# Multi-head attention and an expert layer on one core: all attention first, and seven products instead of eight in the first expert matmul of four batches

## The chip, the core and the metric

The kernel runs on one core of a Trainium2 chip. The core has a matrix engine (TensorE, PE below), a vector engine (VectorE, DVE), a scalar engine that evaluates functions (ScalarE, ACT), a general engine (GpSimd, POOL) that here issues the input transfers, and a queue engine (SyncE, SP) that issues output transfers. They run side by side and wait for each other through semaphores. Matmuls write to PSUM banks; DVE and ACT read them. The metric is the device time of one execution in microseconds (us).

## What is computed

The inputs are q, k, v of 8 batches, 12 heads, 448 tokens and 64 numbers per head, in float32, and two weight matrices, 768 x 2048 and 2048 x 768. Cut to what matters:

```python
scores = q @ k.T / sqrt(64)                 # per batch and head, 448 x 448
attn = exp(scores - max); attn /= sum(attn) # softmax over keys
x = (attn @ v), heads side by side          # 3584 x 768
h = x @ w_in                                # 3584 x 2048, "first expert matmul"
out = (h * sigmoid(h)) @ w_out              # 3584 x 768,  "second expert matmul"
```

h * sigmoid(h) is the function Silu. The matmuls run in float16 with float32 accumulation.

## The kernel before

**Attention.** The 12 heads of a batch are three head groups of four. A *unit* is a batch and a head group (batch 0 is cut into two pieces of tokens as well), 27 units in all. K and Q are loaded per unit, turned by DVE (`turn_k`, `turn_q`), and `scores` multiplies 128 keys at a time with 448 queries on 32-row tiles of PE into a pair of PSUM banks of the ring "s" (two pairs). `expo` (L386) lets ACT write the exponentials to a tile E (nine buffers). `attend` (L412) multiplies them with V, and `attend_sums` (L428) with ones for the softmax's denominators, on 32-column tiles. DVE turns and inverts the sums (`inverse`: sT, inv, rdn) and `norm` (L486) writes xT, half the normalised result, in transposed form.

**First expert matmul.** For batches 0 to 5, `ffn1` multiplies one block of 128 columns of w_in with xT: six products over the 768 rows, 448 tokens wide. ACT takes tanh of it (`tanh`, L511; buffers "th", three) and DVE makes (tanh + 1) * h/2 (`gate`, L546), which is Silu. For batches 6 and 7 together (`PB = B - 2`) it is done as a 2 x 2 block product with seven block products instead of eight (`queue_pair`, `pair_product`): the two batches are the rows, the two halves of the columns the columns, the two halves of the 768 the inner index. For each pair of column blocks f and f + 8 there are seven block products of three matmuls each. Sums of blocks of xT (sx, `combine_x`, L592) and of w_in (tw, `combine_w_in`, L610) are made by DVE before, copies of two intermediate results by ACT (`pair_copy`, L647), three additions by DVE (`pair_add`, L650), and ACT's Silu (`silu`, L659) reads the four results. Tanh and exponential share one function table of ACT, Silu needs another; `first_silu` (L656) brings the load forward.

**Second expert matmul.** For every two tiles of 128 tokens (a *quad*, `queue_quad`) it is also a 2 x 2 block product in seven parts (`product`): DVE makes the sums S and in-place differences in G (`combine_g`, L683), ACT copies (L751), DVE adds (L758, L763), ACT or DVE write the result to ost, and SP stores it (in the last quads ACT's queue too). The first quad is done in four plain products (`plain`).

**Column strips.** While attention runs, `wide` (L337) cuts each 128-column product of the expert layer into four strips of 32 columns, which saves a change of tiling between it and the attention products.

**Order.** Nothing is left to an automatic scheduler. A planner in the kernel (`Order`, `Op`, `Ring`) goes through a clock of estimated durations. DVE and ACT take the operation that has been ready longest, corrected by a `bias`; PE takes a score when its operands and buffers are free and `PACE` us have passed since the last (L1475), else expert work from a list `moe`, of which the first 24 entries are looked through (`moe_ready`), or attention products (`av_at`, `run_av`). Buffers are rings in the planner ("m": four single PSUM banks; "s"; E; V; raw K and Q; turned K; T; S; tmp; ost). The buffers "th" have no ring in it. All loads go through POOL's one queue in a fixed order, and one that waits for its buffer holds back those behind it. V lies in two buffers of a whole batch each.

Of the kernel before, what the change touches and what calls it, by code (L numbers as in the profile page):

```python
# [174 lines left out]
def kernel(  # L175
# [28 lines left out]
    NRK, NRQ = 3, 4  # L204
    PACE = 2.6
# [6 lines left out]
    SHY = 0.5  # L212
    TWB, SXB = 4, 4
    PIECES = ((0, 7), (7, TPP))
    NE, NX3, NT_ = 9, 6, 2
# [32 lines left out]
    VT = [const.tile([128, NH, NCH, D], FP16, name=f"V{i}") for i in range(2)]  # L248

    def clear_v(i, hg, low):  # L250
        rows = slice(64, 128) if low else slice(0, 64)
        nc.vector.memset(VT[i][rows, HG * hg : HG * (hg + 1), NCH - 1], 0.0)

    for hg in (1, 2):
        clear_v(1, hg, hg == 1)
# [26 lines left out]
    def load_v(b, hg0, hg1, x):  # L282
        hs = slice(HG * hg0, HG * hg1)
        first, count = X_TOK[form(b, hg0)][x]
        nc.gpsimd.dma_start(  # L285
            out=VT[b % 2][32 * x : 32 * (x + 1), hs, 0:count, :],
            in_=v[b, hs].rearrange("h (i g) d -> i h g d", g=TPP)[
                :, :, first : first + count, :
            ],
        )  # L290
# [16 lines left out]
    def turn_k(b, hg):  # L307
        t = rawk[(b, hg)][:].bitcast(FP32).rearrange("p (g i) -> p g i", i=32)
        kt = sb.tile([128, NCH, 4, 32, 2], FP16, name=f"KT_{b}_{hg}", tag="KT", bufs=3)
# [94 lines left out]
    def attend_mm(a, n, part, c, h, k0, k1, e, start, stop):  # L404
# [3 lines left out]
        if part == 0:  # L408
            w = ones[k0:k1, :]
        else:  # L410
            w = VT[b % 2][k0:k1, HG * hg + h, c, part - 1 :: 2]
# [24 lines left out]
    def attend(ns, part):  # L436
        lone = len(ns) == 1
        if part == 0 and not lone:
            attend_sums(ns)
            return  # L440
        for n in ns:
            a = ps.tile([128, 512], FP32, name=f"a_{n}_{part}", tag="m", bufs=4)
            acc[(n, part)] = a
            for c in range(NCH):
                e = E[(ns[0] if c == NCH - 1 else n, c // per_burst(n))]
                for h in range(HG):
                    attend_mm(
                        a, n, part, c, h, 0, rows_of(n, c), e, c == 0, c == NCH - 1
                    )

    def inverse(ns, step, i=0):
        g0, g1 = units[ns[0]][2:]
        shape = [128, g1 - g0, 32]
        if step == 0:
            sT_t[ns[0]] = sb.tile(shape, FP32, name=f"sT_{ns[0]}", tag="sT", bufs=1)
# [41 lines left out]
    def ffn1(b, f, t0, t1):  # L497
        h = ps.tile([128, 512], FP32, name=f"h_{b}_{f}_{t0}", tag="m", bufs=4)
        for cc in range(NDC):
# [7 lines left out]
        h_t[(b, f, t0)] = h  # L507

    def tanh(b, f, t0, t1):
        th = sb.tile([128, t1 - t0], FP16, name=f"th_{b}_{f}_{t0}", tag="th", bufs=3)  # L510
# [29 lines left out]
    def gate(b, f, t0, t1):  # L540
        r = b % 2
        cut = 6 * 128 - S if b % 4 == 1 else S
        for lo, hi, dst, at in ((0, cut, G, S * r), (cut, S, X, -cut)):
# [21 lines left out]
    PB = B - 2  # L565
    c_t, sx_t, tw_t, pp_t, pf_t = {}, {}, {}, {}, {}

    def old_buffer(name, home, cols):

        if home == "V":  # L570
            t = VT[name[:2] == "sx"].rearrange("p h c d -> p (h c d)")
        else:
            t = sb.tile([128, HG, S], FP16, name=name, tag="E", bufs=NE)
            t = t.rearrange("p h s -> p (h s)")
        return [
            t[:, 3 * cols * i : 3 * cols * (i + 1)].rearrange("p (c t) -> p c t", c=3)
            for i in range(2 if home == "V" else 1)
        ]

    def combine_x(m):  # L580
        if m < 4:
            made = old_buffer(f"sx_{m}", "V" if m == 3 else "E", S)
            for i, t in enumerate(made):
                sx_t[m + i] = t
        x = {(r, i): x3(PB + r, 3 * i) for r in range(2) for i in range(2)}
        a, b, op = {
            1: (x[1, 0], x[1, 1], ALU.add),
            2: (sx_t.get(1), x[0, 0], ALU.subtract),
            3: (x[0, 0], x[1, 0], ALU.subtract),
            4: (x[0, 1], sx_t.get(2), ALU.subtract),  # L590
        }[m]
        nc.vector.tensor_tensor(out=sx_t[m], in0=a, in1=b, op=op)  # L592
# [5 lines left out]
    def combine_w_in(m, f0):  # L598
        if (m, f0) not in tw_t:
            made = old_buffer(f"tw_{m}_{f0}", W_HOME.get((m, f0), "E"), 512)  # L600
            for i, t in enumerate(made):
                tw_t[(m + i, f0)] = t
        x = {(i, j): w_in_part(i, j, f0, f0 + 4) for i in range(2) for j in range(2)}
        a, b, op = {
            1: (x[0, 1], x[0, 0], ALU.subtract),
            2: (x[1, 1], tw_t.get((1, f0)), ALU.subtract),
            3: (x[1, 1], x[0, 1], ALU.subtract),
            4: (x[1, 0], tw_t.get((2, f0)), ALU.subtract),
        }[m]
        nc.vector.tensor_tensor(out=tw_t[(m, f0)], in0=a, in1=b, op=op)  # L610

    W_HOME = {(1, 0): "V"}
    PBANK = {1: "A", 2: "A", 6: "B", 7: "B", 4: "B", 5: "C", 3: "C"}

    def pair_product(f, m):
        if m in (1, 5):
            pp_t[(f, PBANK[m])] = ps.tile(
                [128, 512], FP32, name=f"f_{f}_{m}", tag="m", bufs=4
            )[:, 0:S]
        elif m == 6:  # L620
            two = ps.tile([128, 2, 512], FP32, name=f"f_{f}_{m}", tag="s", bufs=2)
            pp_t[(f, "B")], pp_t[(f, "D")] = two[:, 0, 0:S], two[:, 1, 0:S]
        x = {(r, i): x3(PB + r, 3 * i) for r in range(2) for i in range(2)}
        lo, at = f // 4 * 4, slice(128 * (f % 4), 128 * (f % 4 + 1))
# [3 lines left out]
            3: (sx_t.get(4), w_in_part(1, 1, f, f + 1)),  # L628
        }.get(m, (None, None))
        if a is None:  # L630
            i = {4: 4, 5: 1, 6: 2, 7: 3}[m]
            a, w = x[1, 1] if m == 4 else sx_t[i], tw_t[(i, lo)][:, :, at]
        for c in range(3):
            wide(
# [8 lines left out]
    def pair_copy(f, name, at):  # L643
        tag, n = {"p": ("rq", NRQ), "q": ("rk", NRK)}[name]
        t = sb.tile([128, TPP * D], FP16, name=f"{name}_{f}", tag=tag, bufs=n)
# [12 lines left out]
    def silu(f, r, x):  # L658
        nc.scalar.activation(  # L659
            out=G[:, f, S * r : S * (r + 1)],  # L660
            in_=pp_t[(f % HF, x)],
            func=AF.Silu,
            scale=2.0,
        )
# [22 lines left out]
    def product(qd, m):  # L687
# [6 lines left out]
        if BANK[m] == m:  # L694
            pr_t[(qd, m)] = ps.tile([128, 512], FP32, name=f"p_{qd}_{m}", tag="m", bufs=4)
        for f in range(HF):
# [80 lines left out]
    rk_ring, rq_ring, v_ring = Ring(NRK), Ring(NRQ), Ring(2)  # L777
    kt_ring, t_ring = Ring(3), Ring(NT_)
# [11 lines left out]
    def plan_v(b, hg0, hg1):  # L790
        made = []
        for x in range(4):
            ring = v_ring if (x == 0 and hg0 == 0) else None
# [79 lines left out]
    quads, fourth = [], []  # L873

    def queue_ffn1(b, g0, g1):
        t0, t1 = 32 * g0, 32 * g1
        for f in range(NFF) if b == 0 else [x for f in range(HF) for x in (f, f + HF)]:

            def run(f=f):
                op = Op("PE", NDC * mm(t1 - t0), lambda: ffn1(b, f, t0, t1), tail=PE_OUT)  # L880
# [4 lines left out]
                od.on_pe(op, "full")  # L885
# [31 lines left out]
    pair_todo = [(m, f0) for f0 in (0, 4) for m in (1, 2, 3, 4)]  # L917

    def plan_pair():
        while pair_todo and not od.pool:  # L920
            m, f0 = pair_todo[0]
            if (m, f0) in W_HOME:
                if not v_ring.can(1, od.now):
                    return
                v_ring.take()
            elif (m - 1, f0) not in W_HOME:
                if qk_seq or not e_ring.can(1, od.now):
                    return
                e_ring.take()
            pair_todo.pop(0)  # L930
            pair_w[(m, f0)] = od.add(
                Op(
                    "DVE",
                    0.98,
                    lambda m=m, f0=f0: combine_w_in(m, f0),
                    [pair_w[(k, f0)] for k in {2: (1,), 4: (2,)}.get(m, ())],
                    TWB + f0,
# [3 lines left out]
    def queue_pair():  # L941
        xs = {(r, c): x_op[(PB + r, c, 0)] for r in range(2) for c in range(NDC)}
        v_ring.take()
        e_ring.take(2)
        od.add(
            Op(
                "ACT",
                2.7,
# [597 lines left out]
```

## Time and profile before

| | |
|---|---|
| time, median of 3 runs | 394.65 us (394.5 to 394.73) |
| the profiled execution: time / span | 394.84 / 392.9 us |
| mean granted clock of PE | 0.999 |
| busy: PE, DVE, ACT, POOL | 386.2, 274.1, 253.1, 83.6 us |
| idle of ACT before E, most of it for scores | 22.5 us |
| ACT's second table load | 1.28 us, at 300 us |
| last attention product / first seven-product work | about 303.7 / 316.0 us |

The span runs from the first to the last instruction. A line of a group gives the line in the kernel, engine, operation, what it writes and reads, shape, count, then busy time and mean length of one in ns, and the engine's idle time before them with what ended it. The chain is the work that ended last, followed back. PE's ends are modelled, and instructions of an engine that follow each other closely overlap, so that mean lengths add up to more than the busy time.

### The profile page before, as it was taken

The page shows a single profiled execution, that of the slowest core. Times are in us where ns is not written, and L with a number is a line of the kernel's source. Part 1 is how long each engine was busy: PE and PEld are TensorE (multiplying, and loading weights), DVE is VectorE, ACT ScalarE, POOL GpSimd, SP SyncE. Part 2 cuts the span into 40 slices and gives each one's busy share as a digit, 9 for nine tenths or more (in the row PEclk, how much of TensorE's full clock was granted, in tenths as well). Part 3 has the DMA queues.
Part 4 walks back from the last instruction along what each step waited for, and adds up shares of the span by engine and source line. Part 5 has one row for each costly group of instructions (what it writes and reads, how often), then busy time and mean ns, then how long its engine had stood idle before and what let it go on. Part 6 is the DMA issues. An engine that isn't in the chain of part 4 may idle for free.

```text
span 392.9 us, 14583 instructions
## 1 busy us (share of the span) xinstructions
PE 386.2 (98%) x6343; PEld 213.1 (54%) x6343; DVE 274.1 (70%) x576; ACT 253.1 (64%) x404; POOL 83.6 (21%) x153
## 2 busy tenths in 40 slices
PE   8999999999999999999999999999999999999995
PEld 7667774444556444555455544445445555555663
DVE  3477676999967488964699576996879945457332
ACT  4988885596872886753874759867695246763221
POOL 6632547206051041230060150600000000000000
PEclk9999999999999999999999999999999999999999
DMA  8999999909067236293091291711100131001343
GB/s 117 205 210 210 163 178 173 201 8 140 11 93 154 57 49 96 42 183 86 3 126 39 70 182 37 102 21 42 46 2 13 34 79 40 0 3 29 94 110 90
DMA packets 35599, 34.76 MB, mean 88 GB/s; under 512 B 11600, under 2 KB 34000, under 8 KB 35536
## 3 DMA queue, kind: packets, MB, share of 16 engines
q0 software_dynamic: 24784, 22.82, 38.8%
q1 hardware_dynamic: 9984, 10.24, 9.7%
q8 instruction: 49, 0.80, 0.9%
q10 hardware_dynamic: 768, 0.79, 0.8%
q14 instruction: 14, 0.11, 0.1%
HBM read 45.61 MB, written 11.01 MB: 144 GB/s over the span
## 4 chain that ended last, share of the span: by engine, by line
PE 95%; DVE 2%; ACT 1%; ACTq 0%; issue 0%; DVEq 0%
PE h L337 29%; PE p L337 28%; PE s L349 13%; PE a L412 10%; PE f L337 8%; PE o L337 3%; PE z L1452 2%; PE a L428 2%; ACT E L386 1%; DVE p L758 1%; DVE tw L610 0%; ACTq L746 0%; DVE T L397 0%; ACT ost L754 0%; DVE rdn L470 0%
## 5 line engine op out<-in xcount | busy, mean ns | idle before, releaser
L386 ACT ACTIVATE E<-s 128x896 f16<-128x896 f32 (+1 forms) x172 | 149.9, 915 | 22.5 <-PE s L349 21.5
L337 PE MATMUL h<-xT,w_in_t 128*32 128x448 f16 (+1 forms) x2112 | 119.3, 345 | 0.0
L337 PEld LDWEIGHTS <-w_in_t 128*32 128x32 f16 (+1 forms) x2184 | 72.8, 97 | 56.7 <-issue 16.4
L511 ACT ACTIVATE th<-h 128x448 f16<-128x448 f32 (+1 forms) x112 | 54.3, 494 | 31.3 <-PE h L337 23.4
L337 PEld LDWEIGHTS <-G 128*32 128x32 f16 (+1 forms) x1352 | 54.5, 97 | 36.3 <-issue 5.2
L546 DVE SCALAR_TENSOR_TENSOR G<-th,h 128x448 f16<-128x448 f16 (+2 forms) x112 | 55.1, 508 | 17.0 <-ACT th L511 15.6
L337 PE MATMUL p<-w_out_t,G 128*32 128x384 f16 (+1 forms) x1016 | 65.5, 326 | 0.7 <-DVE xT L486 0.4
L349 PE MATMUL s<-rq,KT 32*128 32x448 f16 (+4 forms) x864 | 57.0, 342 | 0.5 <-ACT E L386 0.4
L285 POOL DMA_DIRECT2D V<-in_v_dram x88 | 48.5, 563 | 19.7 <-DMA w_out_t<-in_moe_w_out_dram 6.3
L754 ACT COPY ost<-p 128x384 f32<-128x384 f32 x39 | 18.7, 480 | 48.5 <-PE p L337 34.1
L272 POOL DMA_DIRECT2D rq<-in_q_dram x27 | 15.0, 556 | 143.0 <-PE s L349 110.9
L412 PE MATMUL a<-E,V 128*32 128x448 f16 (+2 forms) x864 | 41.2, 333 | 0.0
L337 PE MATMUL p<-D,S 128*32 128x384 f16 (+1 forms) x544 | 37.5, 327 | 0.0
L486 DVE SCALAR_TENSOR_TENSOR xT<-a,rdn 128x448 f16<-128x448 f32 (+1 forms) x54 | 29.3, 564 | 9.3 <-PE a L412 8.0
L349 PEld LDWEIGHTS <-KT 32*128 32x128 f16 (+2 forms) x864 | 17.5, 99 | 29.0 <-issue 27.4
L412 PEld LDWEIGHTS <-V 128*32 128x32 f16 (+1 forms) x864 | 21.5, 97 | 16.5 <-issue 4.1
L397 DVE TENSOR_TENSOR T<-T,E 128x1792 f16<-128x1792 f16 x20 | 21.7, 1087 | 12.2 <-ACT E L386 12.2
L337 PEld LDWEIGHTS <-S 128*32 128x32 f16 (+1 forms) x544 | 20.7, 97 | 14.9 <-issue 2.3
L397 DVE TENSOR_TENSOR T<-E,E 128x1792 f16<-128x1792 f16 x20 | 21.7, 1083 | 7.5 <-ACT E L386 7.5
L659 ACT ACTIVATE G<-f 128x448 f16<-128x448 f32 x32 | 16.2, 547 | 8.4 <-PE f L337 8.3
L320 DVE STREAM_TRANSPOSE KT<-rk 128x256 f32<-128x256 f32 (+3 forms) x48 | 16.6, 384 | 5.1 <-DMA rk<-in_k_dram 5.0
L337 PE MATMUL p<-D,G 128*32 128x384 f16 (+1 forms) x272 | 19.1, 326 | 0.0
(130 smaller groups left out, 309.2 us busy)
## 6 DMA issues: line engine op xcount, KB each, us to landing
out_dram<-ost SPq DMA_DIRECT2D x208, 48.0 KB, 1.7
rk<-in_k_dram POOLq DMA_DIRECT2D x24, 224.0 KB, 5.5
rq<-in_q_dram POOLq DMA_DIRECT2D x21, 224.0 KB, 5.8
w_in_t<-in_moe_w_in_dram POOLq DMA_DIRECT2D x6, 512.0 KB, 11.4
w_out_t<-in_moe_w_out_dram POOLq DMA_DIRECT2D x4, 768.0 KB, 13.1
V<-in_v_dram POOLq DMA_DIRECT2D x43, 64.0 KB, 4.8
V<-in_v_dram POOLq DMA_DIRECT2D x40, 48.0 KB, 5.2
out_dram<-ost ACTq DMA_DIRECT2D x16, 48.0 KB, 1.8
```

The source lines that it names most:

```text
L285: nc.gpsimd.dma_start(out=VT[b % 2][32 * x : 32 * (x + 1), hs, 0:count, :], in_=v[b, hs].rearrange("h (i g) d -> i h g d", g=TPP)[:, :, fi ...
L320: nc.vector.transpose(out=pairs[:, x:y, 0:count], in_=t[:, first : first + count * (y - x)].rearrange("p (x c) i -> p x c i", c=count),)
L337: nc.tensor.matmul(out=out[at], lhsT=lhsT[:, at], rhs=rhs, **flags)
L349: nc.tensor.matmul(out=pS[p0 : p0 + 32 * (x1 - x0), h % 2, at : at + nq], lhsT=KT[(b, hg)][32 * h : 32 * (h + 1), c, x0:x1, :, e], rhs=QT[ ...
L386: nc.scalar.activation(out=E[(n, w)][0:kr, 2 * y : 2 * y + 2, 0:nk], in_=pS_t[(n, w, y)][0:kr, :, 0:nk], func=AF.Exp, scale=attn_scale,)
L397: nc.vector.tensor_tensor(out=T[n], in0=T[n] if step else E[(n, 0)], in1=E[(n, step + 1)], op=ALU.add,)
L412: nc.tensor.matmul(out=a[32 * h : 32 * (h + 1), 0:nq], lhsT=w, rhs=e[k0:k1, h, at : at + nq], start=start, stop=stop,)
L486: nc.vector.scalar_tensor_tensor(out=x3(b, cc)[:, cc % 3, 32 * g0 : 32 * g1], in0=acc[(n, part)][:, 0:nq], scalar=0.5, in1=rdn_t[n].rearra ...
L511: nc.scalar.activation(out=th, in_=h_t[(b, f, t0)][:, 0 : t1 - t0], func=AF.Tanh)
L546: nc.vector.scalar_tensor_tensor(out=dst[:, f, at + lo : at + hi], in0=th_t[(b, f, t0)][:, lo - t0 : hi - t0], scalar=1.0, in1=h_t[(b, f, ...
L659: nc.scalar.activation(out=G[:, f, S * r : S * (r + 1)], in_=pp_t[(f % HF, x)], func=AF.Silu, scale=2.0,)
L754: nc.scalar.copy(out=ost(qd, i, j), in_=bank(qd, m))
```

## The change

1. *Seven products for four batches.* `PB` becomes 4: batches 4, 5 and 6, 7 are two pairs. In the first pair the column blocks 5, 6, 7 and 13, 14, 15 (`EVEN`) stay plain, with tanh and gate, and run while attention is still on or just after. The seven products run only when no score and no attention product is left, and undivided, not in strips. A Silu that straddles the buffers G and X (batch 5) is written in two pieces.
2. *Attention first.* `PACE` goes from 2.6 to 1.5 us, and the catch-up of the pace from 4 to 8. Plain products and products of the second matmul are planned in parts of two matmuls or blocks, between which scores may come (`in_parts`). The two units of a pair are attended one after the other (`av_seq`, `lead`).
3. *Buffers.* V is kept per head group in four buffers (V of batch 0 in the later buffer of D5). xT gets 8 instead of 6 buffers, th 2 instead of 3, sT shares the buffers of rdn. The sums tw are made for two column blocks each, in the freed buffers of V, of turned K and of E; the third of them overwrites w_in in place once nobody needs it. The sums sx lie in E and T buffers.
4. *Order within the seven products:* 1, 5, 6, 2, 3, 7, 4 instead of 1, 5, 6, 2, 7, 3, 4; the sums of a quad are planned by halves; the additions' and copies' bias is stronger; the Silu's table load waits for all exponentials and tanhs.

The diff, cut to its core:

```diff
-    NRK, NRQ = 3, 4
-    PACE = 2.6
+    NRK, NRQ, NKT, NV, NTH = 3, 4, 3, 4, 2
+    PACE = 1.5
...
-    SHY = 0.5
-    TWB, SXB = 4, 4
+    SHY = 0.6
+    TWB, SXB, FAR = 2, 2, 8
-    NE, NX3, NT_ = 9, 6, 2
+    NE, NX3, NT_ = 9, 8, 2
...
-    VT = [const.tile([128, NH, NCH, D], FP16, name=f"V{i}") for i in range(2)]
+    VS = [const.tile([128, HG, NCH, D], FP16, name=f"V{i}") for i in range(NV)]
...
+    def v_of(b, hg):
+        if b:
+            return VS[(NG * b + hg) % NV]
+        whole = W_[5].rearrange("p f m -> p (f m)")
+        return whole.rearrange("p (h c d) -> p h c d", h=NH, c=NCH)
...
-            sT_t[ns[0]] = sb.tile(shape, FP32, name=f"sT_{ns[0]}", tag="sT", bufs=1)
+            sT_t[ns[0]] = sb.tile(shape, FP32, name=f"sT_{ns[0]}", tag="rdn", bufs=2)
...
-        th = sb.tile([128, t1 - t0], FP16, name=f"th_{b}_{f}_{t0}", tag="th", bufs=3)
+        th = sb.tile([128, t1 - t0], FP16, name=f"th_{b}_{f}_{t0}", tag="th", bufs=NTH)
...
-    PB = B - 2
+    PB, EVEN = 4, (5, 6, 7)
...
         for c in range(3):
-            wide(
+            nc.tensor.matmul(
                 out=pp_t[(f, PBANK[m])],
...
+    def silu(b0, f, r, x):
+        for lo, hi, dst, at in halves_of(b0 + r):
+            nc.scalar.activation(
+                out=dst[:, f, at + lo : at + hi],
+                in_=pp_t[(f % HF, x)][:, lo:hi],
+                func=AF.Silu,
+                scale=2.0,
+            )
...
+    PROD_AT, FFN1_AT = 2, 2
+
+    def in_parts(n, size, columns, emit, done, at=0):
+        to = min(at + size, n)
+        op = Op("PE", (to - at) * mm(columns), lambda: emit(at, to), tail=PE_OUT)
+        od.on_pe(op, "full")
+        if to == n:
+            done(op)
+        else:
+            moe.insert(
+                0, (list, 0, lambda: in_parts(n, size, columns, emit, done, to), ())
+            )
...
+    def plan_silu():
+        if silu_op or av_seq or any(ffn1_left[b] for b in range(PB + 2)):
+            return
+        deps = [x for n in range(NU - 2, NU) for x in exp_op[n]]
+        deps += [x for b in (PB - 1, PB, PB + 1) for f in range(NFF) for x in g_op.get((b, f), ())]
+        silu_op.append(od.add(Op("ACT", 1.4, first_silu, deps, -5)))
+
+    def queue_pair(b0):
+        xs = {(r, c): x_op[(b0 + r, c, 0)] for r in range(2) for c in range(NDC)}
         for f in range(HF):
-            queue_pair_f(f, xs)
+            if b0 != PB or f not in EVEN:
+                queue_pair_f(b0, f, xs)
...
             def deps():
+                if qk_seq or av_seq:
+                    return [None]
...
-        for m in (1, 5, 6, 2, 7, 3, 4):
+        for m in (1, 5, 6, 2, 3, 7, 4):
             queue(m)
...
-        av_seq += [(ns, part) for part in range(3)]
+        av_seq.append((ns, 0))
+        av_seq += [([n], part) for n in ns for part in (1, 2)]
+        lead[ns[-1]] = ns[0]
...
-                pace["next"] = min(max(pace["next"], od.now - 4), od.now) + (
+                pace["next"] = min(max(pace["next"], od.now - 8), od.now) + (
                     PACE if u0[0] > EAGER else 0.0
                 ) * len(qk_seq[0][2]) / 2
```

## The prediction

> **What bounds the kernel now.** I read the page's busy times first, then the chain that ended last, the waits of TensorE (PE), the stretches, and last the groups by shape. Busy times and chain, from the page:
>
> ```profile
> PE 386.2 (98%) x6343; PEld 213.1 (54%) x6343; DVE 274.1 (70%) x576; ACT 253.1 (64%) x404; POOL 83.6 (21%) x153
> PE 95%; DVE 2%; ACT 1%; ACTq 0%; issue 0%; DVEq 0%
> ```
>
> PE carries 95% of the chain. The view of waits has only three lines for it; the first is the 1.0 us start, the others are these:
>
> ```profile
> PE p L337 <- DVE xT L486: 0.4, 1, 0.4
> PE s L349 <- ACT E L386: 0.4, 1, 0.4
> ```
>
> So nothing but PE's own instructions can be shortened with effect. Three stretches show how hard VectorE (DVE) and ScalarE (ACT) can work beside a full PE (the second column is the length, then the busy us of PE, PEld, DVE, ACT, POOL):
>
> ```profile
> 76.00:129.00 53.00, 52.85 (x1124) 27.53 (x1120) 44.30 (x96) 35.69 (x56) 13.07 (x24) 1.00 0.51 85
> ...
> 280.00:303.00 23.00, 23.00 (x482) 11.30 (x474) 20.48 (x46) 16.58 (x26) 0.00 (x0) 1.00 0.01 3
> ...
> 322.00:355.00 33.00, 33.00 (x179) 17.34 (x178) 17.33 (x32) 23.17 (x48) 0.00 (x0) 1.00 0.06 16
> ```
>
> With DVE at 89% (20.48 of 23) and ACT at 72%, PE still has no gap; in the seven-product stage it has none with ACT at 70%.
>
> **The PE work removed.** What one 128-wide product costs comes from the chain in order of time:
>
> ```profile
> 91.06 2.27 PE h L337 x48
> ...
> 321.96 28.38 PE f L337 x150
> ```
>
> Forty-eight 32-column strips are 12 products of 448 columns: 2.27/12 = 0.189 us. The 150 undivided products of the seven-product stage: 28.38/150 = 0.189 us. Strips and whole products cost the same, so it is worth nothing that fewer are cut into strips; only the count matters. Counted in the built order, the first expert matmul has 744 such products before (480 as strips, 192 halves = 96, 168 in seven-product form) and 729 after (330 as strips, 30 whole, 192 halves, 273 in seven-product form). Each pair of column blocks (f and f+8) that changes form drops from 24 products to 21; five more pairs do (batches 4 and 5, three stay plain). 15 x 0.189 = **2.84 us less on PE**. Every other PE group (scores, attention, second matmul) has the same count. Changes between row, column and full tiling, which cost about 0.11 us (2.38 us for the same 48 strips right after a score, 2.27 otherwise), number 205 before and 204 after: nothing.
>
> **What it moves to ACT and DVE.** These rows price it:
>
> ```profile
> L386 ACT ACTIVATE E<-s 128x896 f16<-128x896 f32 x156 | 136.0, 915 | 21.1 <-PE s L349 20.3
> L511 ACT ACTIVATE th<-h 128x448 f16<-128x448 f32 x80 | 43.8, 547 | 28.7 <-PE h L337 21.7 <-issue 2.6 <-ACT th L511 2.6
> L546 DVE SCALAR_TENSOR_TENSOR G<-th,h 128x448 f16<-128x448 f16 x48 | 28.5, 613 | 7.2 <-ACT th L511 6.6
> L659 ACT ACTIVATE G<-f 128x448 f16<-128x448 f32 x32 | 16.2, 547 | 8.4 <-PE f L337 8.3
> L650 DVE TENSOR_TENSOR f<-f,q 128x448 f32<-128x448 f32 x16 | 10.0, 632 | 7.0 <-PE f L337 6.1
> L647 ACT COPY p<-f 128x448 f32<-128x448 f32 x8 | 4.4, 545 | 1.4 <-PE f L337 1.3
> L656 ACT ACT_TABLE_LOAD x1 | 1.3, 1283 | 0.0
> ```
>
> Per changed pair ACT gives up four tanhs (2.19 us) and gets two copies and four Silus (3.27 us): 5 x 1.08 = 5.4 us more; the ten Silus that batch 5 has to write in two pieces add about 0.2 us each. DVE gives up four gates (2.45) and gets three additions (1.90), and pays four more sums of xT at 0.85 us. Both totals move by under 8 us and neither engine is full, so in the sum this is nothing; the cover is PE's own 21 x 0.189 = 3.97 us per pair, against 3.3 to 3.6 us of ACT. If ACT fell behind there, each pair would add the difference, which is negative.
>
> **Attention earlier.** The pace between scores falls from 2.6 to 1.5 us. Priced with the rows, the built order has 175 us of PE work between the first score of unit 9 and that of unit 26, before 216. From 76 to 280 us the trace has DVE busy for 157.8 and ACT for 143.7 of 204 us (77% and 70%). In the same stretch of units the ratio of DVE's work to PE's rises from 187/216 to 166/175 (mean durations, which overlap), ACT's from 165/216 to 148/175. Scaled by that, DVE goes to about 85% and ACT to about 78%. Both lie near the 89% and 72% at which PE had no gap from 280 to 303 us. I take 0 and keep 0 to 3 us. Where two plain products stand between scores, the period is 2.89 us in both kernels (2.38 + 0.51).
>
> **The buffer of tanh, three to two.** The order's planner has no ring for it, so ACT can now wait for a gate that it does not foresee, and the exponentials queued behind it wait too, then PE. ACT's and DVE's instructions in order of time show one case (start, length):
>
> ```profile
> 292.57 0.55 ACT L511 ACTIVATE th<-h 128x448 f16<-128x448 f32 x1
> 293.41 0.54 ACT L511 ACTIVATE th<-h 128x448 f16<-128x448 f32 x1 [0.29 <-ACT th L511]
> ...
> 295.49 0.55 ACT L511 ACTIVATE th<-h 128x448 f16<-128x448 f32 x1
> ```
>
> ```profile
> 295.46 0.48 DVE L546 SCALAR_TENSOR_TENSOR G<-th,h 128x320 f16<-128x320 f16 x1
> 295.86 0.28 DVE L546 SCALAR_TENSOR_TENSOR X<-th,h 128x128 f16<-128x128 f16 x1
> ```
>
> The tanh of 295.49 is two behind that of 292.57, whose gate ends at 296.14: with two buffers it would start 0.65 us late. Doing this for all 112 tanhs gives 11 late ones, together 4.0 us, eight of them before 57 us, where the order of PE is the same in both kernels. Ends 0 and 4.0 us; ACT idles a third of the time and PE's waits for ACT are 0.4 us in all, so most is absorbed: I take 0.5.
>
> **The hand-over to seven products.** Before, PE waited 0.45 us at 306 us for xT, as the last attention fed the next work at once. Now plain products of batch 5 stand between the last attention and the first seven-product work, whose batches were normalised long before: minus 0.45. In its place comes the table load. It now stands in ACT's order right behind the first two copies of the stage, in front of the third (p_4_1): 1.28 us and a first Silu of 0.21. From the end of what that copy reads PE has four groups of three products (0.57 us each) before it needs the copy, 2.3 us against 1.5 of load and 0.55 of copy; I reckon 0.3 exposed, ends 0 and 1.5.
>
> Here a rule of the Trainium skill says more than the row. ScalarE: Activation LUTs, section "What ACT_TABLE_LOAD costs", gives the load 1283 ns and a drain of about 1380 ns behind it, 2.66 us for each switch. The trace agrees on the first figure and shows no second: the first Silu began at 301.25 us, as the load of 299.96 us ended. By the Trainium skill the exposed end would be 2.7 instead of 1.5 us.
>
> **Loads.** V's four buffers hold a head group each, and one POOL queue carries K, Q and V in turn; a V that waits for its buffer holds back the next K and Q. In the built order at least 23 us of PE work lie between the attention that frees the buffer and the score that needs that K, against a landing of 5.5 us: nothing. If the cover went, each unit would lose what exceeds it. V of batch 0 in the buffer of D5, and the transposed sums in the buffers of rdn, only order DVE behind itself: nothing.
>
> **The sum.** The profiled execution took 394.84 us (span 392.9 and 1.94 around it), 0.19 above the median. -2.84 - 0.45 + 0.5 + 0.3 = -2.5: 392.35 for it, **392.2 us** as a median. All the small terms at their good ends give 391.4.
>
> **Rivals.**
> 1. Not faster: the tanh buffer. If all 4.0 us reach PE instead of 0.5: 392.2 + 3.5 = 395.7. For it: DVE is denser now, so gates come later. Against: the PE waits above. It makes the kernel slower by over 0.2% from 3.8 us of exposed waits.
> 2. DVE bounds the hand-over. Between the sums of the last attention units and the last plain gate, DVE has 15.5 us of work (rows) against 13.3 us of PE's; were none of it overlapped, 2.2 us return: 394.4. Against: DVE instructions that follow each other overlap (the mean durations of all add up to 305 us, its busy time is 274).
> 3. The table load is bare: 1.5 us instead of 0.3: 393.4. Against: before, nobody waited for it; but then PE had products to run without ACT. By the Trainium skill's 2.66 us it would be 394.5, no change.
>
> **How the numbers follow.** Forecast 0.60, first rival 0.20, second 0.11, third 0.09. A measurement of this kernel tells about 0.2% (0.8 us) from no change. Faster: forecast and third rival, 0.69; same: the second, 0.11; slower: the first, 0.20. The range goes from 390.9, where PE's gaps of the first 58 us also close (56.38 us busy, so 0.6 us besides the start), to 396.0, just beyond the first rival; about one in ten lies above, less below. The forecast's own range is 391.2 to 393.2.
>
> **What would show it.** Right: PE busy about 383 us, 729 products, hardly a wait of PE on ACT or DVE between 70 and 260 us, the third copy of the first seven-product stage not followed by an idle PE. Wrong: PE waits for E (scores) or a bank in the plain products of batches 1 to 3, ACT waiting at tanh for DVE by microseconds, or a gap of PE above 1 us around the table load.

## The result

The changed kernel takes 392.98 us (median of 6 runs, 392.73 to 393.21) against 394.69 us for the kernel before (394.41 to 394.77): a ratio of 0.9958, with a 95% interval of 0.9945 to 0.9971. It is faster by 0.42%, that is 1.7 us where 2.5 were forecast. In a later set of runs on another chip the same two kernels stood at 393.24 and 394.58 us, ratio 0.9967 (0.9955 to 0.9979). The profiled execution took 392.73 us with a span of 391.0. One run of the kernel before (408.97 us, granted clock 0.958) and one of the kernel without parts below (415.88 us, 0.946) fell into a slower state and are left out of medians and ratios.

So the sign and the rough size came out, and about a third of the gain is missing. The rest of this text is about where it went.

### The profile page after: what moved, and what is told of

Same layout as the page of the kernel before. It is cut to its first block, busy times and chain, and to the rows that moved or that the text cites. A ratio compares the mean times of both kernels' runs of the same rounds, so it can differ in the third digit from the quotient of the medians.

```text
span 391.0 us, 13258 instructions
## 1 busy us (share of the span) xinstructions
PE 383.1 (98%) x5662; PEld 208.8 (53%) x5662; DVE 275.0 (70%) x571; ACT 257.7 (66%) x424; POOL 83.7 (21%) x153
## 4 chain that ended last, share of the span: by engine, by line
PE 94%; ACT 2%; DVE 2%; DMA 1%; issue 1%; ACTq 0%; DVEq 0%; POOLq 0%
PE p L345 30%; PE h L345 23%; PE s L357 13%; PE f L650 13%; PE a L420 11%; PE o L345 3%; PE a L436 2%; DMA rk<-in_k_dram 1%; ACT E L394 1%; DVE f L666 1%; PE z L1530 1%; ACTq L763 0%; DVE p L775 0%; ACT G L676 0%; ACT ost L771 0%
## 5 line engine op out<-in xcount | busy, mean ns | idle before, releaser
L394 ACT ACTIVATE E<-s 128x896 f16<-128x896 f32 (+1 forms) x172 | 151.2, 916 | 50.6 <-PE s L357 49.3
L345 PE MATMUL h<-xT,w_in_t 128*32 128x448 f16 (+2 forms) x1542 | 94.4, 342 | 0.0
L345 PEld LDWEIGHTS <-w_in_t 128*32 128x32 f16 (+1 forms) x1542 | 53.5, 97 | 38.2 <-issue 12.6
L345 PEld LDWEIGHTS <-G 128*32 128x32 f16 (+1 forms) x1184 | 52.6, 97 | 39.0 <-issue 8.4
L345 PE MATMUL p<-w_out_t,G 128*32 128x384 f16 (+1 forms) x872 | 66.2, 327 | 0.2
L293 POOL DMA_DIRECT2D V<-in_v_dram x84 | 46.0, 559 | 60.0 <-PE a L420 46.5
L357 PE MATMUL s<-rq,KT 32*128 32x448 f16 (+4 forms) x864 | 56.9, 340 | 1.2 <-ACT E L394 0.8
L559 DVE SCALAR_TENSOR_TENSOR G<-th,h 128x448 f16<-128x448 f16 (+2 forms) x92 | 44.3, 498 | 13.2 <-ACT th L521 13.1
L521 ACT ACTIVATE th<-h 128x448 f16<-128x448 f32 (+1 forms) x92 | 42.2, 485 | 16.8 <-PE h L345 9.8
L345 PE MATMUL p<-D,S 128*32 128x384 f16 (+1 forms) x496 | 37.4, 327 | 0.0
L420 PE MATMUL a<-E,V 128*32 128x448 f16 (+1 forms) x672 | 36.3, 353 | 0.0
L357 PEld LDWEIGHTS <-KT 32*128 32x128 f16 (+2 forms) x864 | 17.6, 98 | 29.6 <-issue 27.2
L676 ACT ACTIVATE G<-f 128x448 f16<-128x448 f32 (+1 forms) x52 | 25.9, 529 | 10.6 <-PE f L650 6.8
L345 PEld LDWEIGHTS <-S 128*32 128x32 f16 (+1 forms) x496 | 20.6, 97 | 14.5 <-issue 2.3
L666 DVE TENSOR_TENSOR f<-f,q 128x448 f32<-128x448 f32 x26 | 16.4, 632 | 15.6 <-PE f L650 14.2
L420 PEld LDWEIGHTS <-V 128*32 128x32 f16 (+1 forms) x672 | 17.1, 96 | 16.4 <-issue 5.8
L650 PEld LDWEIGHTS <-w_in_t 128*128 128x128 f16 x156 | 15.3, 98 | 14.1
```

What stands on the lines that cost most here:

```text
L293: nc.gpsimd.dma_start(out=v_of(b, hg0)[32 * x : 32 * (x + 1), at, 0:count, :], in_=v[b, hs].rearrange("h (i g) d -> i h g d", g=TPP)[:, :, ...
L345: nc.tensor.matmul(out=out[at], lhsT=lhsT[:, at], rhs=rhs, **flags)
L357: nc.tensor.matmul(out=pS[p0 : p0 + 32 * (x1 - x0), h % 2, at : at + nq], lhsT=KT[(b, hg)][32 * h : 32 * (h + 1), c, x0:x1, :, e], rhs=QT[ ...
L394: nc.scalar.activation(out=E[(n, w)][0:kr, 2 * y : 2 * y + 2, 0:nk], in_=pS_t[(n, w, y)][0:kr, :, 0:nk], func=AF.Exp, scale=attn_scale,)
L420: nc.tensor.matmul(out=a[32 * h : 32 * (h + 1), 0:nq], lhsT=w, rhs=e[k0:k1, h, at : at + nq], start=start, stop=stop,)
L521: nc.scalar.activation(out=th, in_=h_t[(b, f, t0)][:, 0 : t1 - t0], func=AF.Tanh)
```

## The profile after

Line numbers have moved: strips and plain products are now L345, seven-product products L650 (they were L337, like everything else in strips), scores L357, E L394, tanh L521, gate L559, copies L663, additions L666, Silu L676, the table load L672. From the page of the changed kernel, the span, the busy times and the shares of the chain that ended last:

```profile
span 391.0 us, 13258 instructions
...
PE 383.1 (98%) x5662; PEld 208.8 (53%) x5662; DVE 275.0 (70%) x571; ACT 257.7 (66%) x424; POOL 83.7 (21%) x153
...
PE 94%; ACT 2%; DVE 2%; DMA 1%; issue 1%; ACTq 0%; DVEq 0%; POOLq 0%
```

PE's busy time fell by 3.1 us (386.2 to 383.1), the span by 1.9. PE is as full as before by its share of the span (98%); in the chain it has 94% instead of 95%, and ACT 2% instead of 1%, with DVE's 2% unchanged. The view of waits of the changed kernel shows PE's own (engine, what waits, for whom; us in total, times, longest; the first line, the 1.0 us of the start, is left out):

```profile
...
PE s L357 <- ACT E L394: 0.8, 2, 0.4
PE p L345 <- ACT 1_3_4110 L768: 0.6, 1, 0.6
PE s L357 <- DVE rq L338: 0.4, 1, 0.4
PE f L650 <- ACT X L676: 0.2, 1, 0.2
PE f L650 <- DVE f L666: 0.2, 1, 0.2
PE f L650 <- ACT G L676: 0.2, 1, 0.2
```

The wait for xT of the kernel before is gone. The three waits for E and rq lie before 54 us. New are a wait for a copy of the second expert matmul, at 166 us, and three small ones in the seven-product work (`f`). They look negligible, 0.6 us together; the chain shows more. Its pieces in order of time, changed kernel, through the two seven-product stages:

```profile
269.54 13.22 PE f L650 x69
282.78 0.64 DVE f L666
283.45 0.44 ACT G L676
...
284.10 2.44 PE f L650 x12
286.57 0.59 DVE f L666
...
287.21 0.65 DVE f L666
...
287.89 0.73 PE f L650 x3
...
318.41 3.99 PE f L650 x21
322.42 0.65 DVE f L666
323.09 0.55 ACT G L676
...
323.68 24.56 PE f L650 x129
```

The chain leaves PE here for an addition of DVE or a Silu of ACT, in the seven-product work. Before, 150 of these products stood in the chain as one piece.

How hard DVE and ACT work beside PE, in stretches of the changed kernel (start and end; length; busy us of PE, PEld, DVE, ACT, POOL with instruction counts; granted clock, DMA share, GB/s):

```profile
76.80:269.50 192.70, 192.04 (x3907) 94.33 (x3908) 162.13 (x313) 142.94 (x209) 45.43 (x84) 1.00 0.49 80
76.80:129.00 52.20, 52.15 (x1076) 25.04 (x1080) 47.21 (x101) 42.46 (x62) 13.79 (x26) 1.00 0.54 85
...
269.50:288.60 19.10, 18.65 (x98) 9.38 (x96) 16.10 (x31) 15.04 (x36) 0.00 (x0) 1.00 0.01 1
318.40:352.70 34.30, 34.14 (x183) 17.70 (x181) 17.48 (x31) 23.89 (x49) 0.00 (x0) 1.00 0.06 14
```

Through the attention DVE is busy 162.13 of 192.7 us, 84%, and ACT 74% (about 85% and 78% were foreseen), and PE lacks 0.66 us in all, of which the copy at 166 us is 0.61. Even at 90% of DVE and 81% of ACT (first 52 us) PE is full. In the first seven-product stage, with DVE at 84% and ACT at 79%, it lacks 0.45 us; in the second, with 51% and 70%, 0.16.

**An account by waypoints.** The first loads make the start of a run vary (the first attention sum begins between 66.2 and 67.4 us in the profiles), and the stores at the end a little too. To compare kernels more finely I measure, in the instructions of PE in order of time, from the first attention sum (`a<-T,half`) to the end of the last seven-product product: 287.94 us before (66.70 to 354.64), 286.39 after, and 286.41 in the second profile of the same kernel. That is 1.55 us less, where PE's work shrank by 15 x 0.189 = 2.84. Counted from start to start, with 0.189 us for a product of 448 columns and 0.162 for a quad product of 384, the two seven-product stages of the changed kernel are 1.7 us longer than their work (1.2 of it in the first); before, the one stage was 0.25 longer. The difference, 1.4, covers the 1.3 that are missing. The attention part loses nearly as much to changes of tiling and waits as before (about 17.6 us in both, within 0.2).

Of the 1.7 us, 1.65 lie before six products, which start late by 0.16, 0.39, 0.39 and 0.22 us in the first stage (at 276.34, 284.10, 287.89 and 292.42 us) and by 0.33 and 0.16 in the second (at 323.68 and 351.98). All six are the product 4 of their pair of column blocks.

## The experiments

Times are medians; the ratio is to the kernel before on the same chip, with its 95% interval. "Waypoints" is the length just defined.

| run | median us | ratio | waypoints us |
|---|---|---|---|
| before | 394.58 to 394.69 | 1 | 287.94 |
| changed kernel, again | 393.24 | 0.9967 [0.9955, 0.9979] | 286.41 |
| before, two tanh buffers | 395.72 | 1.0024 [1.0015, 1.0033] | 288.59 |
| changed, three tanh buffers | 392.98 | 0.9956 [0.9943, 0.9969] | 286.43 |
| changed, first pair all plain | 394.91 | 1.0007 [0.9998, 1.0016] | 288.09 |
| changed, two table loads more | 395.89 | 1.0027 [1.0015, 1.0039] | 288.90 |
| changed, Silu of D behind product 4 | 391.75 | 0.9925 [0.9913, 0.9937] | 284.79 |
| changed, products 7, 3, 4 as before | 392.75 | 0.9948 [0.9936, 0.9960] | 285.47 |
| changed, no plain blocks in the first pair | 395.32 | 1.0017 [1.0008, 1.0025] | 288.0 |
| Silu behind product 4, two plain pairs | 393.39 | 0.9965 [0.9953, 0.9977] | 286.04 |
| Silu behind product 4, nothing in parts | 401.0 | 1.0158 [1.0144, 1.0173] | 293.94 |
| Silu behind product 4, pace 4.0 | 413.86 | 1.0489 [1.0466, 1.0511] | 307.49 |
| before, Silu behind product 4 | 394.64 | 1.0001 [0.9992, 1.0009] | 287.95 |

### The changed kernel again

No edit; it shares a chip with the runs on product 4 and the one without plain blocks.

> The kernel after once more, on the same chip as the next three: 0.4% faster than before, 393.0 us.

393.24 us, and 286.41 on the waypoints, 0.02 from the first profile. What is missing is not the chance of one run.

### The tanh buffers, from both sides

In the kernel before, two buffers instead of three:

```diff
-        th = sb.tile([128, t1 - t0], FP16, name=f"th_{b}_{f}_{t0}", tag="th", bufs=3)
+        th = sb.tile([128, t1 - t0], FP16, name=f"th_{b}_{f}_{t0}", tag="th", bufs=2)
```

> The kernel before with two buffers for tanh instead of three, nothing else. Theory (ACT's idle time takes up the late tanhs): 394.7 us, same as before within 0.2 us, with waits of tanh for DVE on ACT of up to 4 us in all but no new wait of PE. Rival (the smaller ring reaches PE): up to 4.0 us more, 398.7 us; already 395.5 us would speak for it.

In the changed kernel, three instead of two:

```diff
-    NRK, NRQ, NKT, NV, NTH = 3, 4, 3, 4, 2
+    NRK, NRQ, NKT, NV, NTH = 3, 4, 3, 4, 3
```

> The kernel after with three buffers for tanh again. Theory: 393.0 us, as the kernel after, though ACT's 5.4 us of waits at tanh for DVE shrink. Rival (the ring is what the forecast lost): 392.2 us or less.

The first took 395.72 us, 1.0 us more than the kernel before; that it would cost nothing was wrong. Its view of waits has ACT standing at tanh for DVE, a line that the kernel before does not show, and PE's timeline has the wait for xT grown from 0.45 to 0.63 us:

```profile
ACT th L511 <- DVE G L546: 3.1, 5, 2.1
...
307.29 1.46 PE L337 MATMUL p<-w_out_t,G 128*128 128x384 f16 x8 [0.63 <-DVE xT L486]
```

The orders of PE are the same in both, so the traces show where the 0.65 us on the waypoints arise. At 203 us a tanh stands 2.05 us for a gate and holds back the exponentials behind it (203.63 us against 202.47 before). DVE's work slips with them, an addition of the second expert matmul comes at 215.17 instead of 214.13, and by 216 us PE has lost about 0.45. At 296 us another tanh is late, and with its gate the last norm of DVE, which gives the 0.19 at xT. The rest of the 1.0 us is not traced.

The changed kernel has 5.4 us of such waits at tanh, and yet a third buffer gave it nothing: 392.98 us, the same median, 286.43 against 286.39 us. In its order 4.3 of the 5.4 us lie in the plain blocks of batch 5, from 258 us on, behind the last exponentials (254.25 us), where nothing of PE's depends on them at once; the others are four waits of 0.26 or 0.27 us before 57 us. So the same loss of a buffer is worth 1 us in one order and 0 in the other; the first rival (4.0 us of late tanhs) is refuted for this kernel.

### The second pair of batches back to eight products

```diff
-    PB, EVEN = 4, (5, 6, 7)
+    PB, EVEN = 4, tuple(range(HF))
```

All else of the change stays (order of attention, buffers, parts); 15 products come back.

> The kernel after with all column blocks of batches 4 and 5 plain: 15 products of 448 columns more on PE, and no first seven-product stage; attention first, V by head group and all buffers stay. Theory: 15 x 0.189 = 2.84 us more PE work, less about 1.0 us that the first seven-product stage lost in gaps: 393.0 + 1.8 = 394.8 us, that is, the kernel before. Rival (the gain comes from attention first and the buffers): 393.0 us, no change. Second rival (the stage lost nothing): 395.8 us.

394.91 us, as the theory had it, and no different from the kernel before (ratio 1.0007, 0.9998 to 1.0016); on the waypoints 288.09 against 287.94. So attention first, the smaller rings, the new buffers and the new order of products in the one stage left neither cost nor bring anything in sum; single terms of them may cancel. The whole gain comes from the 15 products, and it is 288.09 - 286.39 = 1.7 of their 2.84 us. The missing 1.1 us is the 1.2 that the first seven-product stage loses.

### The table load, three times instead of once

```diff
         nc.scalar.activation(out=t, in_=zeros[:, 0:1], func=AF.Silu)
+        nc.scalar.activation(out=t, in_=zeros[:, 0:1], func=AF.Exp)
+        nc.scalar.activation(out=t, in_=zeros[:, 0:1], func=AF.Silu)
```

> The kernel after with ACT's function table loaded three times instead of once where the Silus begin (Silu, Exp and Silu of one element each), some 1.5 us more on ACT for each extra pair of instructions. Theory (one load is hidden with over 1 us to spare; PE had no gap until 10 us behind it): two more loads, 3.0 us of ACT, show in part, 1 to 2.5 us: 394.0 to 395.5 us. Rival (the load is already bare): the full 3.0 us, 396.0 us. If a load also drained the engine for 1.4 us each time, 398 us or more.

In the changed kernel the one load is hidden. ACT's timeline there:

```profile
270.71 0.53 ACT L663 COPY q<-f 128x448 f32<-128x448 f32 x1
271.26 1.28 ACT L672 ACT_TABLE_LOAD   x1
272.55 0.20 ACT L672 ACTIVATE first_silu<-zeros 128x1 f16<-128x1 f16 x1
272.66 0.51 ACT L663 COPY p<-f 128x448 f32<-128x448 f32 x1
```

and PE's products follow each other through it. The copy p_4_1 is done at 272.66 + 0.51 = 273.17 us; PE's next product into the bank that it reads stands in these six:

```profile
274.48 1.30 PE L650 MATMUL f<-xT,w_in_t 128*128 128x448 f16 x6
```

So 1.3 us are to spare. With two more loads, 395.89 us, 2.9 more than the changed kernel for 2 x (1.28 + 0.21) = 3.0 us more of ACT. By its median alone this is the rival's number; on the waypoints it is 2.5, the upper end of the theory. Timeline of that run, ACT and then PE:

```profile
272.03 1.28 ACT L672 ACT_TABLE_LOAD   x1
273.55 1.28 ACT L673 ACT_TABLE_LOAD   x1
275.07 1.28 ACT L674 ACT_TABLE_LOAD   x1
...
277.04 1.61 PE L650 MATMUL f<-xT,w_in_t 128*128 128x448 f16 x6 [1.62 <-ACT p L663]
```

The cover that the prediction counted (four groups of three products) is there, so its 0.3 us of exposure are 0. It is wider than reckoned because the load begins at 271.26 us, before PE is done with what the copy reads (272.2). Of the 3.0 us on top, the same six products start 1.8 us late (1.62 as shown idle time), which is 3.0 less the 1.3 to spare; two more waits, of 0.3 and 0.4 us, follow behind it, as ACT has not caught up. The third rival (a bare load) is refuted. The Trainium skill, ScalarE: Activation LUTs, section "What ACT_TABLE_LOAD costs", puts a drain of about 1380 ns behind the load's 1283. The trace agrees with the load (1.28 us) and not with the drain: the loads begin 1.52 us after each other, so 0.24 us are left between them for the one-element function.

### Product 4 and the Silu in front of it

The gap at 283 to 284 us in the timeline of the changed kernel, all engines but the weight loads:

```profile
281.44 1.30 PE L650 MATMUL f<-sx,w_in_t 128*128 128x448 f16 x6
...
282.58 0.73 PE L650 MATMUL f<-sx,tw 128*128 128x448 f16 x3
282.78 0.63 DVE L666 TENSOR_TENSOR f<-f,q 128x448 f32<-128x448 f32 x1 [0.49 <-PE f L650]
...
283.15 0.73 PE L650 MATMUL f<-xT,w_in_t 128*128 128x448 f16 x3
...
283.45 0.44 ACT L676 ACTIVATE G<-f 128x320 f16<-128x320 f32 x1 [0.69 <-DVE f L666]
...
283.78 0.27 ACT L676 ACTIVATE X<-f 128x128 f16<-128x128 f32 x1
...
284.10 0.73 PE L650 MATMUL f<-xT,tw 128*128 128x448 f16 x3 [0.23 <-ACT X L676]
```

The PE lines are, in order, products 3 and 7 of one pair of column blocks (the six matmuls), 6 and 2 of the next pair, and product 4 of the first at 284.10. Products follow each other every 0.57 us; this one came 0.95 us after its predecessor. A stall of 0.38 us is shown as 0.23 of idle, because PE's ends are modelled and the last group's end overlaps the next start.

Product 4 adds into bank B. Banks B and D are the two halves of one PSUM tile, `two`. Product 7 adds into B as well; DVE adds q to that and writes the sum to D (282.78). ACT then writes the Silu of D in two pieces, as batch 5 straddles G and X, and that Silu stands before product 4 in the order, since it was queued when product 7 was. Product 4 starts as the Silu's second piece ends. The addition, whose operand B product 4 changes, is done at 283.41, in time. The Silu of D reads nothing that product 4 writes; but it reads the same tile. That the shared tile is why the program lets one wait for the other is argued from the code; no run gave B and D tiles of their own. Order 1, 5, 6, 2, 7, 3, 4 had product 3 between them; the new order 1, 5, 6, 2, 3, 7, 4 has not. In the built orders, 6 of the 13 products 4 of the changed kernel wait for ACT's Silu of D, of the 8 before only one. The 6 are the six that the trace shows late; the other 7 wait for DVE's addition alone, and none of them is late. (At 287.89 us the profile names an addition of DVE, which ends together with the Silu's second piece at 287.84; the program waits for the Silu.) The edit queues the Silu of D behind product 4:

```diff
                 elif m == 7:
                     read("v", "DVE", lambda: pair_add(f, "D", "B", "q"), [op], rk_ring.give)
-                    gate_of(1, 1, "D", [done["v"]], None)
                 elif m == 3:
                     gate_of(1, 0, "C", [op], m_ring.give)
                 else:
+                    gate_of(1, 1, "D", [done["v"], op], None)
                     gate_of(0, 1, "B", [op], s_ring.give)
```

> The kernel after, with the Silu of the fourth result (D) put behind product 4 in the order, so that product 4 does not wait for it. Theory (the first seven-product stage loses its microsecond where product 4 waits for ACT's two-piece Silu of D, which lies in the same PSUM tile as B): the gaps of PE at 284.1 and 287.9 us go, 0.4 us or more faster, 392.6 us or less. Rival (ACT or DVE is simply full in that stage): the gaps move to the next product, 393.0 us or more.

391.75 us (391.53 to 391.92), 1.5 less than the changed kernel beside it and 0.7% less than the kernel before: the fastest of all, and it beats both. All three waits of `f` are gone from its view of waits, and its chain has the stages in one piece:

```profile
270.23 18.16 PE f L650 x96
288.39 1.30 PE p L345 x8
...
317.96 29.51 PE f L650 x156
```

Ninety-six products take 18.16 us, 0.189 each; in the changed kernel the same 96 reach from 269.54 to 288.62 (the next piece of `p`), 19.08 us. Product 4 follows in its place after 0.57 us, with the Silu of D behind it (its first piece is the second of the two instructions at 284.46, its second piece the last line):

```profile
283.69 0.73 PE L650 MATMUL f<-xT,w_in_t 128*128 128x448 f16 x3
284.26 0.73 PE L650 MATMUL f<-xT,tw 128*128 128x448 f16 x3
284.46 1.01 ACT L676 ACTIVATE G<-f 128x448 f16<-128x448 f32 x2 [1.16 <-PE f L650]
...
285.36 0.27 ACT L676 ACTIVATE X<-f 128x128 f16<-128x128 f32 x1
```

This also answers the rival that ACT or DVE is simply too full there: from 270.2 to 288.4 us of this kernel DVE is busy for 15.87 and ACT for 15.11 of 18.20 us (87% and 83%), more than in the changed kernel, and PE lacks nothing.

On the waypoints it gains 287.94 - 284.79 = 3.15 us on the kernel before. That is the prediction's 2.84 for the products, 0.45 of the wait for xT, 0.2 of a stall that the one stage had before (at 317.33 us), less the 0.61 of the copy at 166 us: 2.9 of 3.15 are named.

The other way to part them is the old order of products:

```diff
-                first = {5: 1, 6: 5, 3: 6, 7: 3, 4: 7}.get(m)
+                first = {5: 1, 6: 5, 7: 6, 3: 7, 4: 3}.get(m)
...
-        for m in (1, 5, 6, 2, 3, 7, 4):
+        for m in (1, 5, 6, 2, 7, 3, 4):
```

> The kernel after with the old order of the seven products, 7 before 3, so that product 3 stands between product 7 and product 4. Theory: product 4 has 0.57 us more cover, the gaps before it go, but product 7 now waits for the second addition: 392.6 to 393.2 us. Rival (the order is not what costs): 393.0 us and the same gaps.

392.75 us, 0.5 less than the changed kernel; 0.94 us on the waypoints, more than half of what the moved Silu gives. In the order built from it two of the 13 products 4 still wait for ACT, and one wait for a Silu of 0.29 us shows in the second matmul.

And the same edit in the kernel before, whose order has product 3 in between:

> The kernel before with the Silu of D put behind product 4, nothing else. In its order product 3 stands between 7 and 4, only one of its eight products 4 waits for ACT, and its seven-product stage loses 0.3 us against its PE work. Theory: at most 0.3 us faster, 394.4 to 394.7 us. Rival (the wait costs per block, whatever the order): 1 us faster, 393.7 us.

394.64 us, ratio 1.0001 (0.9992 to 1.0009), waypoints 287.95 against 287.94: nothing. What the edit repairs is what the change brought.

### The plain blocks at the hand-over

```diff
-    PB, EVEN = 4, (5, 6, 7)
+    PB, EVEN = 4, ()
```

All eight pairs of the first two batches in seven products, 9 products fewer (1.70 us).

> The kernel after with no column block plain: three more pairs of blocks in seven-product form, 9 products fewer. Theory by PE work alone: 9 x 0.189 = 1.70 us faster, 391.3 us, if PE stays full. But the plain blocks are also the work that fills PE while DVE makes the sums of xT and w_in behind the last attention; then PE idles for those sums, four of 0.85 and two of 0.5 us: 391.3 + up to 4 us = 395 us. The theory of the hand-over says the second: slower than 393.0 us.

395.32 us, 2.1 more than the changed kernel. The stretch around the end of the attention:

```profile
253.00:270.00 17.00, 15.43 (x142) 7.61 (x131) 15.98 (x28) 10.12 (x20) 0.00 (x0) 1.00 0.10 25
```

DVE is busy 15.98 of 17 us, 94%, and PE lacks 1.57 us: the sums of xT and w_in come due while DVE still turns and normalises the last attention. This is the second rival; three plain pairs keep it off. It is not the whole loss: 9 products fewer and 2.1 us more make 3.8, and three products 4 that wait for the Silu in the first stage cost 1.0 of the others. With two, on top of the moved Silu:

```diff
-    PB, EVEN = 4, (5, 6, 7)
+    PB, EVEN = 4, (6, 7)
```

> The kernel after with the Silu of D behind product 4, and two plain column-block pairs (6 and 7) in batches 4 and 5 instead of three: 3 products fewer, 0.57 us of PE work. Theory: with three plain pairs the hand-over had no gap, with none it had several; with two it is near the edge. If two still cover DVE's sums: 391.75 - 0.57 = 391.2 us, the fastest so far. Rival (DVE's sums come late): 392 us or more, with PE waiting for DVE at the first seven-product work.

393.39 us, 1.6 more than with three plain pairs and the same Silu edit, though it has 3 products fewer. PE's timeline shows two of the waits, one at the first copy and one at an addition 24 us later:

```profile
267.05 0.73 PE L650 MATMUL f<-xT,w_in_t 128*128 128x448 f16 x3 [0.62 <-ACT p L663]
...
290.97 1.30 PE L650 MATMUL f<-sx,w_in_t 128*128 128x448 f16 x6 [0.58 <-DVE f L666]
```

So three is on the right side of a slope: two plain pairs save 0.57 us of PE and none 1.70, and both cost more than they save.

### Attention's place

Both kernels here have the Silu of D behind product 4, so 391.75 us is the one to compare with. First, plain products and quad products whole, not in parts of two:

```diff
-    PROD_AT, FFN1_AT = 2, 2
+    PROD_AT, FFN1_AT = 8, 6
```

> The kernel after with the Silu of D behind product 4, and plain and second-matmul products planned whole again instead of in parts of two; the first score of the last unit then stands 19 us of PE work later, half way back to where it stood before. Theory (where attention stands is worth nothing by itself, PE is full either way): within 0.8 us of 391.75 us; the wait of 0.6 us for the copy at 166 us may go. Rival (attention first is part of the gain): 393 us or more.

401.0 us, 9.2 more; the theory that the attention's place is worth nothing fell. The last plain product ends at 262.4 us, and PE has only scores left, which wait for ACT's exponentials to free the banks; an addition of DVE is then 1.2 us late as well. From its view of waits, and two stretches:

```profile
PE s L357 <- ACT E L394: 4.5, 8, 1.0
PE f L650 <- DVE f L666: 1.2, 1, 1.2
```

```profile
265.00:270.00 5.00, 2.69 (x34) 0.64 (x28) 2.02 (x2) 3.69 (x5) 0.00 (x0) 0.76 0.00 0
270.00:275.00 5.00, 4.75 (x57) 3.56 (x58) 4.90 (x9) 2.97 (x4) 0.00 (x0) 0.55 0.02 5
```

PE is idle for 2.31 of 5 us, and then its granted clock falls to 0.55, so that the attention that could run at last runs slower: 64 strips of E and V take 4.60 us there, 48 of them 2.45 at full clock, which is 3.27 for 64. Of the 8.7 us that the span gained against the Silu edit alone, PE's busy time takes 4.0 (382.6 to 386.6) and its idle time 4.7.

Second, the pace of the scores:

```diff
-    PACE = 1.5
+    PACE = 4.0
```

> The kernel after with the Silu of D behind product 4, and a pace of 4.0 us between scores; parts stay. The last unit's first score again stands 19 us later, by another way. (A pace of 2.6 instead of 1.5 builds the very same program, so the pace itself is no part of the change's effect.) Theory: 391.75 us within 0.8 us. Rival (attention first is part of the gain): 393 us or more.

413.86 us, 22.1 more, by the same picture drawn out:

```profile
PE s L357 <- ACT E L394: 9.4, 18, 0.9
...
260.00:290.00 30.00, 22.81 (x240) 8.72 (x243) 19.01 (x30) 19.80 (x24) 0.00 (x0) 0.66 0.10 15
```

In the changed kernel the seven products wait until no score and no attention product is left. Attention must therefore end before the plain work does; if it does not, PE has nothing to put between scores. Coming early brings nothing (first pair all plain: no change), coming late costs much. And it is not the pace that made it early: with 2.6 in place of 1.5 the planner of the changed kernel writes the identical order, and with 1.5 the order of scores of the kernel before stays where it was. The parts of two account for about half of it: without them the first score of the last unit stands half way back to its old place. What moved the rest was not tried; the xT buffers, eight instead of six, are a candidate.

## Why the prediction was right, and where it was not

- **The 15 products, -2.84 us: right.** Undivided and in strips a product costs 0.189 us in all kernels. The kernel with the Silu moved gets the whole amount on the clock (394.58 - 391.75 = 2.83), the one with the first pair plain shows that the rest of the change gains nothing in sum.
- **Moved ACT and DVE work, "in the sum this is nothing; the cover is PE's own 21 x 0.189 = 3.97 us per pair, against 3.3 to 3.6 us of ACT": this is the step that failed.** It compared throughput per pair, and that comparison holds (ACT at 79%, DVE at 84% in the stage). What it left out is the order inside a pair: product 4 next after product 7 in its pair, with the Silu of D between them on a tile that both touch. The term, put at nothing, measured 1.4 us more loss in these stages than before; moving the Silu gives back 1.5 us on the median. The change list in the text ahead of the prediction has this reordering as its item 4; the prediction gave it no term.
- **Attention earlier, 0: right in size, wrong in cause.** DVE at 84% and ACT at 74% with a full PE are the 85% and 78% foreseen. But it put this down to the pace, which does nothing here, and it missed what an early attention is for: without it the kernel is 9 to 22 us slower.
- **Tanh buffers, +0.5: 0 in this kernel,** 1.0 us in the kernel before. The row that it used (a tanh 0.65 us late at 295 us) is a case of the kernel before; there that tanh cost PE 0.19 us, and the one at 203 us the rest that the traces show. In the changed order no exponential stands behind the late ones.
- **Hand-over, -0.45 for xT: came,** but a wait of 0.61 us for a copy at 166 us was not foreseen and takes it back. It arose in the attention part, where the copy stands behind two tanhs and an exponential on ACT, and no run was spent on it; the run without parts does not have it, but much else differs there.
- **Table load, +0.3: 0,** hidden with 1.3 us to spare; the prediction's own terms, 2.3 us of cover against 1.5 + 0.55, had left nothing bare either.
- **Rivals.** The first (tanh) fell. The second (DVE at the hand-over) does not happen with three plain pairs and does with none; with two, PE stands at the hand-over for a copy of ACT (0.62 us). The third (bare load) fell.

The sum with what the runs measured: -2.84 - 0.45 + 0.61 + 0 + 0 + 1.4 = -1.3 us, beside 1.55 on the waypoints and 1.7 on the medians; about 0.3 us of gain in the attention part has no name. The 1.4 is what the seven-product stages lose against their PE work after (1.7) less before (0.25). That the forecast came within 0.8 us is in part luck: the two terms that did not come, 0.5 and 0.3, stood in for more than half of the one that was left out. The forecast of 2.5 was right in sign because the large term is a count of products on the engine that bounds the kernel.

## What to carry to other kernels

When an engine is full, throughput ("3.6 us of ACT beside 4.0 of PE") does not yet clear a stage in which neighbours in the order touch the same tile: look for the reader queued between two writers, and put it behind the second writer if the data allow it. A move that brings nothing by itself can still be the condition of another one, so test it by pushing it the other way, together with what it serves. What a smaller buffer ring cost depended, in the two orders tried, on what stood behind the late instruction on its engine, not on how late it was.

## What the chip showed that I had not expected

PE's granted clock fell to 0.55 with no idle stretch of PE over 1.0 us, as its modelled ends show them. In the run without parts, PE's waits from 263 to 269 us are 1.00, 0.44, 0.82, 0.44, 0.83 and 0.22 us, with a few scores between them, and the clock is 0.76 from 265 to 270 us and 0.55 from 270 to 275, when PE was busy again; from 275 us it is 1.00. At pace 4.0 it is 0.66 over 30 us, with waits for E of 0.9 us at most. The Trainium skill, TensorE: Matmul & The Clock Gate, section "What's actually happening", has the clock halved after an idle window of about 3.4 us. The halving agrees with the 0.55; here a busy share of about a half over 5 us, in short pieces, was enough, without any idle window of that length.
